# Attention rows in another order: 768 keys last, 512 keys ahead of it, the short rows between long ones

## The chip, the cores and the metric

The kernel runs on one core of one Trainium2 chip. The metric is the device time of one launch in microseconds (us); the time of a kernel is the median of its runs. The engines are TensorE (PE, with its weight loads as PEld), VectorE (DVE), ScalarE (ACT), GpSimd (POOL) and SyncE (SP).

## What is computed

Three layers run one after the other on 2 sequences of 768 positions and 512 channels: a retention with decay in blocks, a normalised two-layer MLP with 2048 inner channels, and an attention with four experts, of which a gate takes two for each position. The change lies in the last layer alone:

```python
logits = x @ w_gate
topk = np.argpartition(-logits, K, axis=-1)[..., :K]
w = np.exp(sel)                       # of the two taken, then normed
for e in range(E):
    q = x @ wq[e]
    k = x @ wk[e]
    v = x @ wv[e]
    scores = scale * (q @ k.transpose(0, 2, 1))
    scores = np.where(causal, -1000000000.0, scores)
    a = np.exp(scores)                # normed by its sum
    ye = a @ v @ wo[e]
    out += mask[..., None] * w[:, :, kk:kk + 1] * ye
```

## The kernel before

A **row** of attention is a pair (b, t): sequence b and its block t of 128 queries. Because of the causal mask row t has (t + 1) * 128 keys, from 128 (t = 0) to 768 (t = 5). There are twelve rows, and the tuple `ROWS` (line 53) names their order. Each row has four **items**, one for each expert e, so that 48 items pass through a pipeline written out by hand; TensorE's instructions stand exactly in the order in which this code gives them, while the other engines' are ordered by a scheduler.

One turn k of the last loop issues, in this order on TensorE: the scores of item k (`att_s`, L802); pieces of the filler, which are the projections of later blocks (`pv`, L744, and `pj`, L722); the transposes of item k - 5 (`att_t`, L839); in every second turn the product with v of the two items up to k - 7 (`att_av`, L851); in every fourth turn the output projection of the row whose last item is k - 10 (`att_o`, L872). Behind the last score the turns go on without scores until the last row is through.

Between the score and the transpose of an item lies work of the other engines: DVE masks the diagonal block (L804, or L809 for a pair) and takes the row maximum (L805, L811), ACT takes the exponential out of PSUM into `att` (L806, L814), DVE turns the sum into a reciprocal `c` (L825, L826), POOL multiplies by it and by the gate's weight (L829). Behind the transpose ACT copies the result out of PSUM (`aT`, L840); behind the second `av` ACT and DVE split it into two parts (`avs`, L857, L858).

Scores lie in PSUM tiles of two banks called "big", of which there are two. For rows of up to 512 keys two experts share one (a **pair**: mask, maximum and exponentials start when both scores are there); with 640 or 768 keys each expert has a tile of its own. A third tile can be begun when all readers of the first, the exponentials among them, are done:

```python
def ps_big(name):
    return psum.tile([P, 2, 512], F32, tag="big", bufs=2, name=name)
pair = n <= 512
if not pair or e % 2 == 0:
    row["s"] = ps_big(f"s{b}{t}{e}")
```

Everything else of this stage in PSUM (`pv`, `pj`, `t`, `av`, `o`) takes turns in four tiles of one bank, called "mid". The filler has 24 steps, eight for each of three blocks of queries; a row of sequence b may not start before the blocks that it reads are projected, and otherwise the steps are spread over the first 36 turns:

```python
while done < per_blk * (2 * b + t // NTB):
    more[done]()
```

One of a block's eight steps is its gate, some twenty small DVE instructions (L758 to L775).

Of the kernel before, what the change touches and what calls it, by code (L numbers as in the profile page):

```python
# [49 lines left out]
FILL = 36  # L50
AV_AT, O_AT = 2, 5

ROWS = ((0, 0), (0, 1), (0, 2), (0, 3), (0, 4), (1, 2), (0, 5), (1, 5), (1, 1), (1, 4), (1, 3), (1, 0))
LAG = 5
NG = FT // GF
E = 4
# [11 lines left out]
def model(ctx, tc, qkT, kv, lam, g_ln, w12, wat, out):  # L68
# [791 lines left out]
    def att_o(b, t):  # L860
# [3 lines left out]

        halves = 2 if (b, t) == ROWS[-1] else 1
        for j in range(halves):
# [17 lines left out]
    per_blk = len(more) // (NBLK - 1)  # L884
    items = [(b, t, e) for b, t in ROWS for e in range(E)]
    done = 0
# [77 lines left out]
```

## Time and profile before

| | |
|---|---|
| median of 3 runs | 483.04 us (483.02 to 484.16) |
| the profiled execution | 484.76 us, of which 482.8 us are the span from first to last instruction |
| PE busy | 98% of the span |
| DVE, ACT, POOL busy | 70%, 41%, 18% |
| the chain that ended last | PE 85% |

The profile is of one execution. A busy share is a mean over stages; what bounds a stage is read from the waits in it. The chain of work that ended last is followed back from the last instruction; its pieces give what each instruction added to the time.

### The profile page before, as it was taken

How to read it: one execution, taken by the hardware profiler on the slowest of the kernel's cores; microseconds unless marked ns; L12 is line 12 of the kernel's file. 1: busy time of each engine (PE TensorE's matmuls, PEld its weight loads, DVE VectorE, ACT ScalarE, POOL GpSimd, SP SyncE). 2: the span in 40 equal slices, each digit the busy share in tenths (PEclk: the TensorE clock that was granted, in tenths of full speed). 3: DMA queues.
4: the chain of work that ended last, by engine and by line, in shares of the span. 5: the costliest groups of instructions: out<-in, count | busy, mean ns of one | idle time of the engine just before them, and what ended most of it. 6: DMA issues, size and time to landing. Idle time of an engine off the chain costs nothing.

```text
span 482.8 us, 8791 instructions
## 1 busy us (share of the span) xinstructions
PE 472.1 (98%) x3451; PEld 437.9 (91%) x3456; DVE 340.3 (70%) x707; ACT 196.1 (41%) x447; POOL 85.3 (18%) x132
## 2 busy tenths in 40 slices
PE   8899999999999999999999999999999999999996
PEld 4667888999999999999999999999998889898885
DVE  4489688897999796923799925245579676676663
ACT  2326646622233332211233412022346575547672
POOL 5463430000000000000000000000045444334340
PEclk9899999999999999999999999999999999999999
DMA  7877511121334212310222400000000000000111
GB/s 279 331 223 240 196 45 45 45 87 45 113 107 128 90 56 77 98 34 1 87 88 87 132 0 1 1 1 1 0 2 0 24 23 22 24 2 23 45 44 67
DMA packets 10841, 35.18 MB, mean 73 GB/s; under 512 B 1456, under 2 KB 1712, under 8 KB 10800
## 3 DMA queue, kind: packets, MB, share of 16 engines
q1 hardware_dynamic: 10512, 34.49, 21.4%
q8 instruction: 27, 0.44, 0.4%
q10 hardware_dynamic: 288, 0.13, 0.1%
q14 instruction: 14, 0.11, 0.1%
HBM read 31.47 MB, written 3.15 MB: 72 GB/s over the span
## 4 chain that ended last, share of the span: by engine, by line
PE 85%; DVE 5%; issue 3%; DMA 3%; POOL 2%; ACT 1%; SPq 0%; POOLq 0%; DVEq 0%; ACTq 0%
PE h L485 27%; PE y L519 26%; PE pj L722 4%; PE s L802 4%; PE av L851 4%; PE o L872 4%; PE t L839 4%; PE pv L744 3%; PE yf L538 2%; DMA kvn<-in_kv 2%; PE po L373 1%; POOL qd L334 1%; PE sc L326 1%; PE po L366 1%; DMA qk<-in_qkT 1%
## 5 line engine op out<-in xcount | busy, mean ns | idle before, releaser
L485 PE MATMUL h<-xn,w 128*128 128x384 f32 x768 | 140.2, 336 | 0.0
L485 PEld LDWEIGHTS h<-xn,w 128*128 128x128 f32 x768 | 133.4, 188 | 2.8 <-issue 0.8
L519 PE MATMUL y<-hs,w 128*128 128x384 f32 x552 | 99.8, 334 | 0.0
L519 PEld LDWEIGHTS y<-hs,w 128*128 128x128 f32 x552 | 96.1, 188 | 0.0
L504 ACT ACTIVATE hs<-h 128x384 fp32r<-128x384 f32 x50 | 24.5, 490 | 101.7 <-PE h L485 88.3
L736 POOL TENSOR_SCALAR kh<-kh 64x384 fp32r<-64x384 f32 x16 | 8.4, 522 | 300.1 <-DVE qs L730 288.5
L505 DVE SCALAR_TENSOR_TENSOR hs<-h,hs 128x384 fp32r<-128x384 f32 x50 | 27.7, 554 | 41.1 <-ACT hs L504 41.1
L524 DVE TENSOR_TENSOR xT<-xT,y 128x768 f32<-128x768 f32 x30 | 28.5, 950 | 31.6 <-PE y L519 31.6
L829 POOL TENSOR_SCALAR att<-att,c,gw 128x128 f32<-128x128 f32 (+5 forms) x48 | 35.6, 747 | 51.8 <-DVE c L826 16.3
L229 ACT CAST w<-top 128x512 fp32r<-128x512 f32 x32 | 19.8, 620 | 52.3 <-DVE top L223 50.3
L722 PE MATMUL pj<-x,wa 128*128 128x384 f32 x192 | 35.0, 337 | 0.0
L722 PEld LDWEIGHTS pj<-x,wa 128*128 128x128 f32 x192 | 33.4, 188 | 0.0
L840 ACT COPY aT<-t 128x512 f32<-128x512 f32 (+3 forms) x64 | 26.6, 442 | 11.1 <-PE t L839 10.8
L839 PE MATMUL t<-ident,att 128*128 128x128 f32 x168 | 26.2, 275 | 0.5 <-DVE qs L730 0.5
L214 ACT ACTIVATE mag<-raw 128x512 f32<-128x512 f32 x32 | 21.2, 668 | 7.1 <-DVE w L241 7.1
L234 DVE SCALAR_TENSOR_TENSOR mag<-raw,mag 128x512 f32<-128x512 uint32 x32 | 23.2, 726 | 0.6
L851 PE MATMUL av<-aT,v 128*64 128x128 f32 x336 | 23.6, 280 | 0.0
L802 PE MATMUL s<-kh,qs 128*128 128x512 f32 (+3 forms) x64 | 23.3, 365 | 0.0
L238 DVE TENSOR_TENSOR top<-top,w 128x512 f32<-128x512 f32 x32 | 22.9, 715 | 0.0
L223 DVE SCALAR_TENSOR_TENSOR top<-raw,mag 128x512 int32<-128x512 int32 x32 | 21.9, 686 | 0.5
L241 DVE TENSOR_TENSOR w<-top,mag 128x512 fp32r<-128x512 f32 x32 | 21.9, 685 | 0.4
L851 PEld LDWEIGHTS av<-aT,v 128*64 128x64 f32 x336 | 17.8, 136 | 4.4 <-issue 3.9
(128 smaller groups left out, 726.8 us busy)
## 6 DMA issues: line engine op xcount, KB each, us to landing
raw<-in_w SPq DMA_DIRECT2D x32, 512.0 KB, 3.8
qk<-in_qkT SPq DMA_DIRECT2D x12, 512.0 KB, 5.5
kvn<-in_kv SPq DMA_DIRECT2D x12, 512.0 KB, 5.0
out<-os SPq DMA_DIRECT2D x11, 256.0 KB, 2.0
rawa<-in_wat SPq DMA_DIRECT2D x3, 512.0 KB, 3.3
rawa<-in_wat SPq DMA_DIRECT2D x1, 520.0 KB, 4.0
out<-os SPq DMA_DIRECT2D x1, 128.0 KB, 1.7
out<-os ACTq DMA_DIRECT2D x1, 128.0 KB, 1.7
```

Of the source, the lines that this page charges most:

```text
L234: nc.vector.scalar_tensor_tensor(mag, RAW[ft, i][:, :, 0].bitcast(U32), 2.0 ** -52, mag, ALU.mult, ALU.mult)
L485: nc.tensor.matmul(ph[:, :TB], w[:, wi, k, :], xn[:, xi, k, :], start=(i == 0), stop=(i == 11))
L504: LAST.append((nc.scalar.activation(h[:, 0], ph[:, :TB], AF.Relu), nc.vector.scalar_tensor_tensor(h[:, 1], ph[:, :TB], 0.0, h[:, 0].bitcas ...
L505: nc.vector.scalar_tensor_tensor(h[:, 1], ph[:, :TB], 0.0, h[:, 0].bitcast(F32), ALU.max, ALU.subtract)))
L519: nc.tensor.matmul(y[:, j, :TB], w[:, wi, e * P:(e + 1) * P], h[:, xi], start=(f == 0 and i == 0), stop=(f == GF - 1 and i == 2))
L524: nc.vector.tensor_tensor(xv, xv, y[:, :, :TB], ALU.add)
L722: nc.tensor.matmul(ps[:, :TB], w[:, wi, k, :], x2[:, xi, k, :], start=(i == 0), stop=(i == 11))
L802: nc.tensor.matmul(ps[:, c0:c1], q, kk[:, e, c0:c1], start=(i == 0), stop=(i == 1))
L829: nc.gpsimd.tensor_scalar(a[:, :n], a[:, :n], c, gw, ALU.mult, ALU.mult)
L839: nc.tensor.transpose(pt[:, (j - j0) * P:(j - j0 + 1) * P], a[:, j * P:(j + 1) * P], ident)
L840: nc.scalar.copy(aT[:, j0 * P:j1 * P], pt[:, :(j1 - j0) * P])
L851: nc.tensor.matmul(pav[e2 * HD:(e2 + 1) * HD, pr * P:(pr + 1) * P], v[:, j, e * HD:(e + 1) * HD], row["aT"][e][:, j * P:(j + 1) * P], star ...
```

## The change

One line: the order of the twelve rows. The first seven stay. Behind (0, 5) came (1, 5), (1, 1), (1, 4), (1, 3), (1, 0); now come (1, 1), (1, 4), (1, 0), (1, 3), (1, 5). In keys: 768, 256, 640, 512, 128 before, 256, 640, 128, 512, 768 now. The same instructions are issued on each engine, in another order.

```diff
-ROWS = ((0, 0), (0, 1), (0, 2), (0, 3), (0, 4), (1, 2), (0, 5), (1, 5), (1, 1), (1, 4), (1, 3), (1, 0))
+ROWS = ((0, 0), (0, 1), (0, 2), (0, 3), (0, 4), (1, 2), (0, 5), (1, 1), (1, 4), (1, 0), (1, 3), (1, 5))
```

**First place: turn 28, behind the scores of (0, 5).** TensorE before: (1, 5) needs sequence 1's last block of queries, so that a value step and all four projections (two query, two key) stand in a row ahead of its score `s_4465`.

```order
L839 MATMUL t_4342<-ident,att_4149 128x128 x3
L744 MATMUL pv_4347<-wa_2888,x_3_3289 128x260 x12
L722 MATMUL pj_4386<-x_3_3289,wa_2804 128x384 x12
L722 MATMUL pj_4403<-x_3_3289,wa_2841 128x384 x12
L722 MATMUL pj_4424<-x_3_3289,wa_2804 128x384 x12
L722 MATMUL pj_4441<-x_3_3289,wa_2841 128x384 x12
L802 MATMUL s_4465<-kh_3458,qs_3462 128x512
```

TensorE now: (1, 1) comes first and needs no more than is there; the value step stands in turn 28, one projection in turn 31 (`pj_4476`), three in turn 32 ahead of (1, 4)'s score `s_4566`.

```order
L802 MATMUL s_4438<-kh_3458,qs_3461 128x256
L802 MATMUL s_4438<-kl_3459,qs_3461 128x256
L722 MATMUL pj_4476<-x_3_3289,wa_2804 128x384 x12
L839 MATMUL t_4494<-ident,att_4282 128x128 x4
L839 MATMUL t_4500<-ident,att_4282 128x128 x2
L722 MATMUL pj_4504<-x_3_3289,wa_2841 128x384 x12
L722 MATMUL pj_4525<-x_3_3289,wa_2804 128x384 x12
L722 MATMUL pj_4542<-x_3_3289,wa_2841 128x384 x12
L802 MATMUL s_4566<-kh_3458,qs_3462 128x512
```

The block of five filler steps is parted into one, one and three, with scores, transposes and products between.

**Second place: the turns behind the pair of 512 keys, (1, 3) with experts 2 and 3.** TensorE before: the pair's scores are `s_4869`; then come one pair of (1, 0) in the other big tile (`s_4917`) with (1, 4)'s transposes and products, and `s_4974` is the next to need the tile of `s_4869`.

```order
L802 MATMUL s_4869<-kl_3459,qs_3462 128x512
L839 MATMUL t_4905<-ident,att_4770 128x128 x4
...
L802 MATMUL s_4917<-kh_3458,qs_3461 128x128
...
L839 MATMUL t_4929<-ident,att_4803 128x128 x4
...
L851 MATMUL av_4938<-aT_4848,v_3460 64x128
...
L839 MATMUL t_4957<-ident,att_4823 128x128 x4
L872 MATMUL o_4964<-wa_2935,avs_4894 128x512 x6
L802 MATMUL s_4974<-kh_3458,qs_3461 128x128
```

TensorE now: the pair is `s_4835`. Behind it come the transposes and the product of (1, 0), one block each, and (1, 5)'s first score `s_4877` in the other tile; (1, 5)'s second, `s_4901`, takes the tile of `s_4835`.

```order
L802 MATMUL s_4835<-kl_3459,qs_3462 128x512
L839 MATMUL t_4871<-ident,att_4732 128x128
L802 MATMUL s_4877<-kh_3458,qs_3462 128x512
...
L839 MATMUL t_4894<-ident,att_4761 128x128
L851 MATMUL av_4897<-aT_4820,v_3460 64x128
L851 MATMUL av_4897<-aT_4846,v_3460 64x128
L802 MATMUL s_4901<-kh_3458,qs_3462 128x512
```

What stands between the pair and the next user of its tile shrank from a pair of scores, fourteen transposes, ten products and an output projection to one score, two transposes and two products.

DVE now, at the same place: the mask of the pair stands behind the split `avs_4860` of row (1, 4).

```order
L826 RECIPROCAL c_4842<-c_4842 128x1
L858 TENSOR_TENSOR avs_4860<-av_4802,avs_4860 128x256
L809 COPY_PREDICATED s_4835<-tri,fill 128x2x128
L811 TENSOR_REDUCE negm_4778<-s_4835 128x2
L804 COPY_PREDICATED s_4877<-tri,fill 128x128
```

Only behind this maximum do ACT's two exponentials of the pair start.

## Rows read from the trace of the kernel before

**Rows 1.** The page: busy share of each engine; TensorE's clock in tenths, by fortieths.

```profile
PE 472.1 (98%) x3451; PEld 437.9 (91%) x3456; DVE 340.3 (70%) x707; ACT 196.1 (41%) x447; POOL 85.3 (18%) x132
PEclk9899999999999999999999999999999999999999
```

**Rows 2.** Waits of TensorE from 409 us on: us in total, times, longest.

```profile
PE o L872 <- ACT avs L857: 0.5, 1, 0.5
PE o L872 <- DVE kl L734: 0.2, 1, 0.2
```

**Rows 3.** Timeline, start and duration: output projection behind transposes, with and without wait.

```profile
433.45 0.82 PE L839 MATMUL t<-ident,att 128*128 128x128 f32 x6
434.52 1.65 PE L872 MATMUL o<-wa,avs 128*128 128x512 f32 x6 [0.25 <-DVE kl L734]
...
442.58 0.82 PE L839 MATMUL t<-ident,att 128*128 128x128 f32 x6
443.15 1.63 PE L872 MATMUL o<-wa,avs 128*128 128x512 f32 x6
```

**Rows 4.** Timeline: the pair (1, 3), experts 2 and 3, to its second exponential.

```profile
462.59 0.40 PE L802 MATMUL s<-kl,qs 128*128 128x512 f32 x1
463.03 0.44 DVE L809 COPY_PREDICATED s<-tri,fill 128x256 f32<-128x256 int32 x1 [0.30 <-PE s L802]
463.38 0.41 DVE L858 TENSOR_TENSOR avs<-av,avs 128x256 fp32r<-128x256 f32 x1
463.71 1.21 DVE L811 TENSOR_REDUCE negm<-s 128x2 f32<-128x1024 f32 x1
465.01 0.69 ACT L814 ACTIVATE att<-s,negm 128x512 f32<-128x512 f32 x1
465.69 0.68 ACT L814 ACTIVATE att<-s,negm 128x512 f32<-128x512 f32 x1
467.57 0.22 PE L802 MATMUL s<-kh,qs 128*128 128x128 f32 x1
```

**Rows 5.** Chain, start and length of a piece: the pieces that TensorE's path is made of.

```profile
436.17 0.71 PE s L802 x4
438.34 0.90 PE s L802 x4
473.55 0.11 PE t L839
475.05 0.37 PE av L851 x4
477.43 0.38 ACT avs L857
477.86 1.69 PE o L872 x12
```

**Rows 6.** Timeline of DVE in the gate: a slow one, its last.

```profile
424.11 0.70 DVE L765 TENSOR_TENSOR rank<-rank,cmp 128x9 f32<-128x9 f32 x1
428.54 0.17 DVE L775 TENSOR_TENSOR gw<-gw,mx 128x12 f32<-128x12 f32 x1
```

**Rows 7.** Timeline of TensorE around the longest wait, in the retention.

```profile
19.03 1.72 PE L326 MATMUL sc<-qk 64*128 64x128 f32 x16 [1.87 <-DMA qk<-in_qkT]
20.68 1.12 PE L357 MATMUL po<-kvn,kd 128*64 128x64 f32 x16
21.73 1.63 PE L366 MATMUL po<-qd,st 64*64 64x128 f32 x16
25.07 1.16 PE L326 MATMUL sc<-qk 64*128 64x128 f32 x16
32.13 0.69 PE L357 MATMUL po<-kvn,kd 128*64 128x64 f32 x16
32.75 1.09 PE L366 MATMUL po<-qd,st 64*64 64x128 f32 x16
```

**Rows 8.** Window of Rows 7: span, busy (count) of PE, PEld, DVE, ACT, POOL, PEclk, DMA, GB/s.

```profile
20.00:21.00 1.00, 1.00 (x14) 0.78 (x13) 0.55 (x2) 0.63 (x2) 0.67 (x1) 0.50 1.07 418
```

## The prediction, written before the changed kernel ran

> **What bounds the kernel now.** I read the page first: TensorE is busy 98% of the span and its clock is at full speed in all but one fortieth [rows 1]. The engines beside it have room (DVE 70%, ACT 41%). A mean says little about a stage, so I next took TensorE's waits from 409 us on, where the rows of attention that the change moves lie. There are two in some 70 us: 0.2 us for a `kl` of the projections and 0.5 us for the last split of all [rows 2]. The reader is to see that this stage is one unbroken stream of TensorE instructions. The change only permutes them, so their sum stays; what can differ are the waits between them. I therefore went through the new order and asked at each hand-over whether what TensorE waits for is still ready in time.
>
> **Part 1, the filler (turns 28 to 32): about 0.5 us are gained.** Before, five filler steps stand in a row. DVE clears four projections behind them, with the gate's small instructions in between, and is late by the end: the output projection that needs a freed mid tile starts 434.52 - 433.45 = 1.07 us after the transposes ahead of it, and where nothing waits the same two start 443.15 - 442.58 = 0.57 us apart [rows 3]. The wait costs 0.50 us, twice the idle time that its row shows, because the pipeline also drains. Now the gate comes two turns ahead of the first projection, and behind the last one stands a product of 24 matmuls where one of 12 stood. DVE has more time, so I take the whole 0.50 us as gained. The bounds are 0 (the wait comes back at the new place) and 0.5 us. What is late next there is the projection of turn 31: its mid tile is the one of an output projection whose copy now stands on DVE behind most of the gate's instructions, and this is a rival below. The short row (1, 1) costs nothing: its chain runs under the value step and the transposes of (0, 5).
>
> **Part 2, the pair of 512 keys ahead of the row of 768: about 2.1 us are lost.** This is the term on which the forecast hangs. There are two big tiles. The second score of (1, 5) takes the tile of the pair (1, 3) with experts 2 and 3 and cannot begin before both exponentials of that pair have left it.
>
> How long that takes, the pair's rows of before tell [rows 4]: its score ends at 462.59 + 0.40 = 462.99; mask, split and maximum follow on DVE; the exponentials end at 465.69 + 0.68 = 466.37. That is 3.38 us. Handing on to TensorE takes 0.05 us more (the last split ends at 477.43 + 0.38 = 477.81 and its user starts at 477.86 [rows 5]), together 3.43 us.
>
> What TensorE has to do meanwhile: before, 467.57 - 462.99 = 4.58 us pass until the next user of that tile [rows 4], more than 3.43, and nothing waits. Now it is a transpose of one block, a score of 768 keys, a transpose of one block and a product of one block for two experts, at 0.11, 0.71, 0.11 and 0.37 us [rows 5]: 1.30 us. The score is 0.71 where it doesn't follow a product and 0.90 where it does [rows 5]; this one follows a transpose. So TensorE stands still for 3.43 - 1.30 = 2.13 us, and no later wait is there to take it back but the last one, which stays.
>
> Its bounds: the shortest way through mask, maximum and two exponentials alone is 0.44 + 1.21 + 0.69 + 0.68 us and some 0.2 us of hand-overs, 3.2, which leaves a wait of 1.9 us. At the other end, the mask now stands behind the split of row (1, 4) on DVE, which ACT hands on only after the exponentials of the pair before; if its 0.41 us lie wholly ahead of the mask, 3.8 us and a wait of 2.5 us. I take 2.13, the measured row, since it holds the same instructions.
>
> The other hand-overs of the same kind have room. (1, 5)'s third score needs its first one's exponential, and between lie its second score, four transposes and an output projection; (1, 0) comes behind (1, 4) as (1, 3) did before, with the same pieces between.
>
> **Part 3, the drain.** The last row's chain is now that of 768 keys instead of 128, with no scores behind it to cover it. But behind its last score TensorE still has the transposes and products of (1, 3), the output projection of (1, 0) and its own first three heads' transposes. At 0.11 us for each of 26 blocks of transposes, 0.37 for each of eight blocks of products [rows 5] and 436.17 - 434.52 = 1.65 for the projection [rows 3, 5] I estimate 7.5 us. The last item's way to its transpose is, without POOL, about as long as the 3.4 us of the pair. I put it at nothing; if this cover were gone, the rest of that way would lie on the path. The sequence in the last turns, transposes, product, output projection, is the same as before, and so is the end: split, 0.5 us of waiting, the projection in two halves, the copy, the DMA. SP's and ACT's output DMAs keep their number and sizes, and the last full row's DMA is issued earlier against the end than before. Nothing is moved on SP but which row an issue writes.
>
> **The sum.** -0.50 + 2.13 = +1.6 us. The profiled execution took 484.76 us, 1.72 us above the median, and its own time would become 486.4. On the median, 483.04 us, I forecast 484.6 us. With the bounds, +1.4 to +2.5, the forecast's own range is 484.4 to 485.5.
>
> **The rivals.**
>
> *The wait takes TensorE's clock down.* In the retention TensorE stood idle for 1.87 us, and behind it the granted clock was 0.50, the level of 1.2 GHz [rows 8]. The three groups that ran from 19.03 us on took 1.72, 1.12 and 1.63 us, against 1.16, 0.69 and 1.09 us at full clock [rows 7]: 1.53 us more. The new wait is as long or longer. If the same happens, the cost is 1.6 + 1.5 = +3.1 us, 486.1 us. For it speaks the length of the wait; against it, that the matmuls around it are denser than the retention's and that shorter waits left the clock at full speed [rows 1, 2]. The Trainium skill's page "TensorE: Matmul & The Clock Gate" (Part 1: The HAM clock gate) says that there are only two rates and that an idle TensorE is taken down to the half; the trace agrees, with 0.50 behind 1.87 us. [...]
>
> *TensorE doesn't wait: the other side.* If ACT and DVE, with short rows before and after, were through with the pair in 1.30 us, or the tile were free earlier than by its second exponential, only the gain of part 1 would remain: 482.5 us, not slower than before. It decides at 1.30 + 0.50 = 1.8 us from the pair's score to its release: below that, the change is no loss. The instructions alone take 3.0 us [rows 4], which speaks against it.
>
> *The gate holds the first projection.* In turn 31 the projection needs the copy of an output projection that now stands behind some twelve of the gate's instructions on DVE. Before, the gate kept DVE until 428.7 us, with other work between, and one of its small instructions took 0.70 us where another takes 0.17 [rows 6]. The copy is due about 2.1 us after its projection ends; I reckon it to be there just in time. Two instructions so stretched would add 2 * 0.53, some 1 us to the forecast: 485.6 us.
>
> **How the numbers follow.** Chances: forecast 0.45, clock 0.30, no wait 0.15, gate 0.10. The predicted time is the forecast's, 484.6 us. The range leaves out half of the no-wait case below and a sixth or so of the clock case above: 482.7 to 486.5 us. A measurement of this kernel can tell about 0.3%, 1.45 us, from no change: below 481.6 is faster, above 484.5 slower. The forecast lies close to that edge, so a third of its chance counts as the same, with nearly all of the no-wait case: 0.15 + 0.14 = 0.29, and 0.02 for the rest, 0.31. Faster is 0.04, slower 0.65.
>
> **What would show it.** In the profile of the changed kernel: a wait of TensorE at L802 (`s` for an exponential of L814) of about 2 us, some 23 us before the end, and no other above 0.3 us but the last one; the wait at L872 for `kl` gone; the granted clock of the microseconds behind the wait, 1.00 for the forecast and 0.50 for the clock's rival; in turn 31 no wait of `pj` for the copy of L875; and transposes of the last row that wait for no POOL. I am wrong if TensorE runs through the pair without a stop, or if the last row's drain shows waits that part 3 put at nothing.

## The result, and the profile after

The changed kernel takes 486.57 us (486.10 to 486.83), the kernel before 483.03 us in the same comparison: a ratio of 1.0071, with an interval of 1.0058 to 1.0084. It is slower by 3.5 us. The forecast was 484.6 us, its range 482.7 to 486.5; the rival in which the wait takes TensorE's clock down stood at 486.1 us.

The page of the changed kernel, where the profiled execution took 486.52 us with a span of 484.5 us, answers [rows 1]: the busy share of each engine, and TensorE's clock by fortieths of the span.

```profile
PE 471.2 (97%) x3456; PEld 436.9 (90%) x3456; DVE 339.6 (70%) x707; ACT 195.7 (40%) x447; POOL 84.8 (17%) x132
PEclk9999999999999999999999999999999999999989
```

Before, the one slice below full speed was the second, in the retention; now it is the last but one, in the rows that were moved. The waits of TensorE from 400 us on answer [rows 2] (us in total, times, longest):

```profile
PE s L802 <- ACT att L814: 2.2, 1, 2.2
PE o L872 <- ACT avs L857: 0.5, 1, 0.5
```

The wait for `kl` is gone, and a score waits 2.2 us for an exponential. It is the second score of (1, 5), and the timeline shows it with the pair (1, 3) that holds its tile, as [rows 4] did (start, duration, and in brackets the idle time and what ended it):

```profile
456.72 0.39 PE L802 MATMUL s<-kl,qs 128*128 128x512 f32 x1
457.24 0.47 DVE L809 COPY_PREDICATED s<-tri,fill 128x256 f32<-128x256 int32 x1
457.74 1.22 DVE L811 TENSOR_REDUCE negm<-s 128x2 f32<-128x1024 f32 x1
457.96 0.44 PE L851 MATMUL av<-aT,v 128*64 128x128 f32 x4
459.06 0.69 ACT L814 ACTIVATE att<-s,negm 128x512 f32<-128x512 f32 x1 [0.67 <-DVE negm L811]
459.74 0.68 ACT L814 ACTIVATE att<-s,negm 128x512 f32<-128x512 f32 x1
460.56 0.50 PE L802 MATMUL s<-kh,qs 128*128 128x512 f32 x1 [2.16 <-ACT att L814]
461.75 2.91 PE L872 MATMUL o<-wa,avs 128*128 128x512 f32 x6
466.37 0.50 PE L802 MATMUL s<-kh,qs 128*128 128x512 f32 x1
```

The pair's score ends at 457.11 and its second exponential at 460.42: 3.31 us, where [rows 4] gave 3.38. TensorE has work until 457.96 + 0.37 = 458.33 (the 0.37 of [rows 5]) and goes on at 460.56: 2.23 us are lost. Behind the wait the same output projection that takes 1.63 us in [rows 3] takes 2.91. Why, the stretches of one microsecond tell (behind the busy times of PE, PEld, DVE, ACT and POOL stands TensorE's granted clock, then the DMA's share and GB/s):

```profile
461.00:462.00 1.00, 1.00 (x9) 0.95 (x8) 0.43 (x1) 0.39 (x2) 1.00 (x2) 0.85 0.00 0
462.00:463.00 1.00, 1.00 (x4) 0.81 (x4) 1.00 (x3) 0.59 (x1) 0.14 (x1) 0.50 0.00 0
...
464.00:465.00 1.00, 1.00 (x4) 0.77 (x3) 0.30 (x1) 0.36 (x2) 0.53 (x1) 0.50 0.00 0
465.00:466.00 1.00, 1.00 (x9) 0.79 (x7) 0.78 (x4) 0.00 (x0) 0.00 (x0) 0.95 0.00 0
```

From shortly before 462 us to shortly after 465 TensorE runs at 0.50, the 1.2 GHz level, and it is busy all that time: the loss does not show as a wait.

A second, smaller delay is in no list of waits of TensorE's matmuls, since it stands inside a group of transposes:

```profile
447.35 0.37 ACT L814 ACTIVATE att<-s,negm 128x128 f32<-128x128 f32 x1 [0.21 <-DVE c L826]
447.71 0.36 ACT L814 ACTIVATE att<-s,negm 128x128 f32<-128x128 f32 x1
448.06 1.06 ACT L840 COPY aT<-t 128x128 f32<-128x128 f32 x3
447.64 1.06 PE L839 MATMUL t<-ident,att 128*128 128x128 f32 x5
448.37 0.14 PEld L839 LDWEIGHTS t<-ident,att 128*128 128x128 f32 x1 [0.34 <-ACT aT L840]
448.63 0.66 PE L851 MATMUL av<-aT,v 128*64 128x128 f32 x8
...
450.53 0.71 PE L839 MATMUL t<-ident,att 128*128 128x128 f32 x5
451.17 1.31 PE L851 MATMUL av<-aT,v 128*64 128x128 f32 x20
```

Five transposes of (1, 4) with a product behind them take 448.63 - 447.64 = 0.99 us here and 451.17 - 450.53 = 0.64 further on. They need a mid tile back from an `aT` copy, which stands on ACT behind the two exponentials of (1, 0), a row that was not there before. Cost: 0.35 us.

**Where the time is compared.** The traces differ by up to 2 us ahead of the attention (in the profiled execution of before the retention ran partly at half clock [rows 7, 8]), and the code there is the same. So I compare a stretch that all kernels share: from the first score of attention to the start of the last output projection. Its ends, of before and then of after:

```profile
356.22 0.22 PE L802 MATMUL s<-kh,qs 128*128 128x128 f32 x1
```

```profile
354.33 0.22 PE L802 MATMUL s<-kh,qs 128*128 128x128 f32 x1
...
479.60 1.68 PE L872 MATMUL o<-wa,avs 128*128 128x256 f32 x12 [0.53 <-ACT avs L857]
```

Before, 477.86 [rows 5] - 356.22 = 121.64 us; after, 479.60 - 354.33 = 125.27 us; +3.63 us, close to the 3.54 us between the medians. Such a stretch is of one execution each, the profiled one.

### The profile page after: what moved, and what is told of

Same layout as the page of the kernel before. It is cut to its first block, busy times and chain, and to the rows that moved or that the text cites. A ratio compares the mean times of both kernels' runs of the same rounds, so it can differ in the third digit from the quotient of the medians.

```text
span 484.5 us, 8802 instructions
## 1 busy us (share of the span) xinstructions
PE 471.2 (97%) x3456; PEld 436.9 (90%) x3456; DVE 339.6 (70%) x707; ACT 195.7 (40%) x447; POOL 84.8 (17%) x132
## 3 DMA queue, kind: packets, MB, share of 16 engines
HBM read 31.47 MB, written 3.15 MB: 71 GB/s over the span
## 4 chain that ended last, share of the span: by engine, by line
PE 86%; DMA 4%; issue 3%; DVE 3%; ACT 2%; POOL 2%; SPq 0%; POOLq 0%; ACTq 0%; DVEq 0%
PE h L485 27%; PE y L519 26%; PE pj L722 6%; PE s L802 4%; PE av L851 4%; PE t L839 3%; PE o L872 3%; PE pv L744 3%; DMA qk<-in_qkT 2%; PE yf L538 2%; PE po L373 1%; PE po L366 1%; ACT att L814 1%; PE sc L326 1%; DMA kvn<-in_kv 1%
```

## The experiments

Stretch is the one just defined, less the 121.64 us of before. "Before" is the kernel before on the same chip in the same comparison.

| kernel | median, us | before, us | ratio (interval) | stretch, us |
|---|---|---|---|---|
| changed | 486.57 | 483.03 | 1.0071 (1.0058 to 1.0084) | +3.63 |
| seven matmuls in the wait | 484.90 | 482.91 | 1.0040 (1.0026 to 1.0054) | +2.07 |
| four | 485.14 | 482.91 | 1.0045 (1.0030 to 1.0059) | +2.05 |
| two | 485.06 | 483.11 | 1.0038 (1.0025 to 1.0051) | +2.08 |
| (1, 3) without pairs | 483.50 | 483.08 | 1.0013 (1.0004 to 1.0023) | +0.67 |
| tail 256, 128, 640, 512, 768 | 486.83 | 483.08 | 1.0071 (1.0055 to 1.0087) | +3.96 |
| tail 256, 640, 512, 128, 768 | 483.51 | 482.91 | 1.0014 (1.0001 to 1.0027) | +0.41 |
| tail 256, 768, 640, 512, 128 | 483.33 | 482.91 | 1.0009 (0.9998 to 1.0020) | +0.41 |
| 256 early, 768 not last | 483.38 | 483.08 | 1.0008 (0.9998 to 1.0018) | +0.22 |
| 256 early, 768 last | 483.92 | 483.08 | 1.0016 (1.0007 to 1.0025) | +0.97 |
| before, filler over 30 turns | 484.74 | 483.11 | 1.0028 (1.0015 to 1.0041) | +1.83 |

**The clock by itself.** If the half clock is a cost of its own behind the wait, keeping TensorE at work in the wait must give it back and leave the wait's own cost. The matmuls write a tile that nothing reads; `warm` is the kernel's own helper.

```diff
             while done < per_blk * (2 * b + t // NTB):
                 more[done]()
                 done += 1
+            if k == 45:
+                warm(7, "z")
             att_s(b, t, e)
```

> The changed kernel with seven idle matmuls on zeros (128x512, bf16) ahead of the second score of row (1, 5), in the place where TensorE waits for the pair. They belong to no result. Theory (the wait itself costs 2.2 us and the clock that falls behind it another 1.5): TensorE is kept at work for some 1.5 us of the wait, the rest of it is about 0.6 us, the score still starts when the exponentials are through, but the granted clock stays at 1.00 and the output projection behind it takes 1.6 us and not 2.9: 486.57 - 1.5 = 485.0 us. Rival (the projection behind the wait is slow for another reason, as its operands or the other engines, and the clock has no part): 486.6 us, the projection again at 2.9 us.

With seven, the clock stayed at 1.00 in every microsecond of the attention and the time fell by 486.57 - 484.90 = 1.67 us. The stretch fell by 3.63 - 2.07 = 1.56. Four of them:

> As the one with seven, but four idle matmuls: some 0.9 us of the wait are filled and TensorE stands idle for about 1.3 us in one piece. Theory, if an idle of that length leaves the clock alone: 485.0 us as with seven; if it already takes the clock down: 486.5 us with a granted clock of 0.50 behind the wait. The retention of before stood idle for 1.00 us without a fall and for 1.87 us with one, so that I put 60 to 40 on no fall. Rival (clock has no part): 486.6 us at full clock with a projection of 2.9 us.

The wait was then 1.1 us, the clock stayed at 1.00, and the stretch is the same as with seven within 0.02 us, since the exponential and not TensorE sets when the score starts. Two of them were to find the idle time at which the clock falls, after an order (below) had shown a fall behind 1.39 us:

> The changed kernel with two matmuls of no use ahead of the score that waits, so that TensorE stands idle there for about 1.6 us instead of 2.2. With four of them (1.1 us idle) the clock stayed at full speed; in the order with 128 keys ahead of 640 it fell behind an idle of 1.4 us. Theory (the idle's length decides, somewhere between 1.1 and 1.4 us): half clock behind the wait, 486.6 us. Rival (the matmuls between keep the clock up): full clock, 485.1 us.

The timeline around the wait with two:

```profile
458.71 0.11 PEld L104 LDWEIGHTS <-zeros 128*128 128x128 bf16 x2 [0.17 <-issue]
458.71 0.39 PE L104 MATMUL warmz<-zeros 128*128 128x512 bf16 x1
460.94 0.50 PE L802 MATMUL s<-kh,qs 128*128 128x512 f32 x1 [1.84 <-ACT att L814]
462.11 1.63 PE L872 MATMUL o<-wa,avs 128*128 128x512 f32 x6
...
465.18 0.50 PE L802 MATMUL s<-kh,qs 128*128 128x512 f32 x1
```

The idle time of 1.84 us in that row is too long: two weight loads stand at 458.71 and only one matmul, so the trace lacks the record of the second. In the changed kernel's retention three such matmuls take 0.82 us and one takes 0.39, so that they start (0.82 - 0.39) / 2 = 0.22 us apart. The second then ended at about 459.3, and TensorE stood idle for about 1.6 us (an estimate), as I had reckoned. That left the clock alone in all five executions (mean clock 1.000 in each), so the theory of a length between 1.1 and 1.4 us fell. This kernel and the changed one give the price of the half clock best, since they differ in the two matmuls alone: from the score that waited to the fourth score it is 466.37 - 460.56 = 5.81 us in the changed kernel and 465.18 - 460.94 = 4.24 here, 1.57 us more.

**The pair as the cause of the wait.** The order stays, but (1, 3) gives each head a tile of its own, so that the second score of (1, 5) waits for one exponential and not for two behind a common maximum.

```diff
-        pair = n <= 512
+        pair = n <= 512 and (b, t) != (1, 3)
```

(in `att_s` and in `att_c`)

> The row order of the changed kernel stays; each head of row (1, 3) has a big tile of its own instead of two heads sharing one, as the rows of 640 and 768 keys have. The second score of (1, 5) then waits for the mask, the maximum and one exponential of a single head of 512 keys (estimated 1.9 to 2.0 us) against 1.3 us of TensorE's work between. Theory (the wait is the pair's release, and the half clock follows from its length): a wait of about 0.6 us at the score, the clock at full speed behind it, and 483.0 - 0.5 + 0.6 + 0.4 = 483.5 us. Rival (the row of 768 keys as the last costs the time by itself): 485 us or more.

Timeline at the score:

```profile
458.65 0.69 ACT L806 ACTIVATE att<-s,negm 128x512 f32<-128x512 f32 x1 [0.70 <-DVE negm L805]
459.48 0.50 PE L802 MATMUL s<-kh,qs 128*128 128x512 f32 x1 [0.47 <-ACT att L806]
```

The wait is 0.47 us, the clock 1.00 throughout, and the time as expected, 483.50 us. Three of the 3.6 us are gone with the row of 768 keys still at the end and that of 512 still in front of it: that much was the price of the tile that the pair keeps and of the clock behind it, not of the order itself. A part of what is left is again a wait for an exponential, which no row of TensorE's matmuls shows: the first score of (1, 5) starts 457.57 - 457.30 = 0.27 us after the transpose ahead of it, in the changed kernel 456.97 - 456.95 = 0.02 us.

**The short row in front of the 640 keys.** Moving (1, 0) ahead puts the products of the row of 640 keys between the pair and the score that needs its tile.

```diff
-(1, 1), (1, 4), (1, 0), (1, 3), (1, 5)
+(1, 1), (1, 0), (1, 4), (1, 3), (1, 5)
```

> The row of 768 keys stays the last and that of 512 ahead of it, but the row of 128 is moved in front of that of 640: behind (0, 5) come (1, 1), (1, 0), (1, 4), (1, 3), (1, 5). Theory (each wait is the work of TensorE since the tile's last score against its readers' 3.4 us for a pair, 2.1 to 2.3 us for one head of 640): two waits, about 0.5 us at the first score of (1, 3) and about 0.4 us at the second score of (1, 5), since the products and transposes between are now those of the row of 640 keys and not of the row of 128; no half clock; gain of the filler 0.5, drain about 0.5 behind so short a wait: 484.0 us, 483.6 to 484.4. Rival (two long rows in a row at the end cost by themselves): 485 or more, with the wait of some 2 us and the half clock as in the changed kernel.

I was wrong by 2.8 us. The two waits are where they were expected, but longer, and behind the first one the clock fell (TensorE's timeline, DVE's, and a stretch of one microsecond):

```profile
446.82 0.27 PE L802 MATMUL s<-kl,qs 128*128 128x128 f32 x1
450.24 0.80 PE L802 MATMUL s<-kh,qs 128*128 128x512 f32 x1 [1.39 <-ACT att L806]
461.60 0.50 PE L802 MATMUL s<-kh,qs 128*128 128x512 f32 x1 [0.95 <-ACT att L814]
```

```profile
446.89 0.69 DVE L875 COPY os<-o 128x512 f32<-128x512 f32 x1
447.80 0.15 DVE L825 TENSOR_SCALAR c<-ssum 128x1 f32<-128x1 f32 x1 [0.23 <-ACT att L806]
448.07 0.28 DVE L804 COPY_PREDICATED s<-tri,fill 128x128 f32<-128x128 int32 x1
```

```profile
451.00:452.00 1.00, 1.00 (x7) 0.36 (x5) 0.00 (x0) 0.81 (x3) 0.87 (x1) 0.50 0.00 0
```

The head of 640 keys whose tile is wanted ends its score at 446.82 + 0.27 = 447.09, but its mask starts only at 448.07: DVE has the copy of an output projection ahead of it and, behind a short wait for ACT, the reciprocal of the head before. So the release took 450.24 - 447.09 = 3.15 us, where I had reckoned 2.1 to 2.3 from the instructions alone. Of four executions three took 486.83 to 487.11 us, with a mean clock of 0.996 over the span, and one 484.93 with 1.000. One of the three is the profiled one; for the other two the mean doesn't tell where the clock fell, but the fourth shows that the same kernel can go without the fall. Even that one is 0.9 us above the forecast.

**The row of 768 keys as the last, by itself.** Two orders end on it without 512 keys in front:

```diff
-(1, 1), (1, 4), (1, 0), (1, 3), (1, 5)
+(1, 1), (1, 4), (1, 3), (1, 0), (1, 5)
```

> Rows 512 and 128 of the changed order exchanged: ..., 256, 640, 512, 128, 768. The row of 768 keys stays last and the filler stays as changed; the pair of 128 keys now stands ahead of the 768. Theory (all of the loss is the wait for the pair of 512 and the clock behind it; the filler gains 0.5 us and the long last row costs nothing): no wait of s for an exponential above 0.3 us, clock 1.00, 483.03 - 0.5 = 482.5 us. Rival (the drain of a 768-key row at the end costs, or the order at large does): 484 us or more with waits in the last 20 us.

No score waits, but the drain does (timeline):

```profile
469.32 0.60 PE L839 MATMUL t<-ident,att 128*128 128x128 f32 x4
470.10 0.44 PE L839 MATMUL t<-ident,att 128*128 128x128 f32 x2 [0.18 <-ACT aT L840]
470.47 0.44 PE L851 MATMUL av<-aT,v 128*64 128x128 f32 x4
470.84 0.87 PE L839 MATMUL t<-ident,att 128*128 128x128 f32 x6
471.99 0.87 PE L839 MATMUL t<-ident,att 128*128 128x128 f32 x6 [0.28 <-POOL att L829]
472.79 1.53 PE L851 MATMUL av<-aT,v 128*64 128x128 f32 x24
```

The first six transposes take 470.47 - 469.32 = 1.15 us, the twelve behind 472.79 - 470.84 = 1.95; in the changed kernel six take 0.74 and twelve 1.46, without a wait:

```profile
471.27 0.82 PE L839 MATMUL t<-ident,att 128*128 128x128 f32 x6
472.01 1.09 PE L851 MATMUL av<-aT,v 128*64 128x128 f32 x16
473.04 1.53 PE L839 MATMUL t<-ident,att 128*128 128x128 f32 x12
474.50 1.53 PE L851 MATMUL av<-aT,v 128*64 128x128 f32 x24
```

The drain costs 0.41 + 0.49 = 0.90 us there. The stretch, +0.41, is that less some 0.5.

The same comparison with the row of 256 keys moved ahead of (0, 5), first with the tail of before, then with 768 keys last:

```diff
-(0, 5), (1, 1), (1, 4), (1, 0), (1, 3), (1, 5)
+(1, 1), (0, 5), (1, 5), (1, 4), (1, 3), (1, 0)
```

> The tail is that of the kernel before, (1, 5), (1, 4), (1, 3), (1, 0), but the row of 256 keys is moved ahead of (0, 5), into the stretch of the filler: ..., (1, 2), (1, 1), (0, 5), (1, 5), (1, 4), (1, 3), (1, 0). Theory (the 0.5 us of the five filler steps in a row can be had if no tile of scores is needed early anywhere): no wait of a score above 0.3 us, the wait for the projection's copy gone or kept, drain as before: 482.4 to 482.5 us, below the kernel before. Rival (the wait only moves: (0, 5)'s scores now meet the short row, or the filler's block stands in a row as before): 483.0 us or more.

```diff
-(0, 5), (1, 1), (1, 4), (1, 0), (1, 3), (1, 5)
+(1, 1), (0, 5), (1, 4), (1, 3), (1, 0), (1, 5)
```

> As the run with the row of 256 keys ahead of (0, 5), but with the row of 768 keys as the last: ..., (1, 1), (0, 5), (1, 4), (1, 3), (1, 0), (1, 5). No row of 512 keys stands directly ahead of it. The difference to that run is the price of the drain with 768 keys by itself, with no long wait ahead of it that gives the other engines time. Theory: 0.9 us of waits at the last transposes, as in the order that had 128 keys ahead of the 768: 483.4 us. Rival (the drain costs nothing, as the prediction had it): 482.5 us.

The one with 768 keys last is slower by 0.97 - 0.22 = 0.75 us in the stretch and by 0.54 between the medians, with the same two waits in the drain (0.18 and 0.27 us idle). In the one with the tail of before the rival held: the four projections still stand together ahead of a score, with two transposes between, and the wait is at its new place:

```profile
437.79 1.66 PE L872 MATMUL o<-wa,avs 128*128 128x512 f32 x6 [0.44 <-DVE kl L734]
```

**The filler's half microsecond.** Two more tries to have it without the pair. The long rows in falling order behind (1, 1):

```diff
-(1, 1), (1, 4), (1, 0), (1, 3), (1, 5)
+(1, 1), (1, 5), (1, 4), (1, 3), (1, 0)
```

> The order of before with rows 768 and 256 exchanged only: (0, 5), then 256, 768, 640, 512, 128. This is the change's filler part alone: the short row runs first, the filler is parted, the last rows stay as before. Theory: the wait of the output projection for kl is gone, 483.03 - 0.5 = 482.5 us. Rival (the wait for kl moves elsewhere, or the gate on DVE holds the first projection): 483.0 us or above, with a wait of TensorE at pj or t between 420 and 440 us.

The `kl` wait is gone, but the second score of (1, 4) now waits 0.98 us for the last exponential of (1, 5), because only the one- and two-block work of (1, 1) lies between. And the kernel before with its own order, where only the pace of the filler is changed:

```diff
-FILL = 36
+FILL = 30
```

> The kernel before with its own row order; only the filler is spread over 30 turns instead of 36, so that fewer of its steps stand in a row ahead of (1, 5). Theory (the wait at the output projection comes from the five steps in a row and costs 0.5 us): the wait for the projection's copy is gone, nothing else moves, 482.5 us, below the kernel before. Rival (more filler earlier is late somewhere else): 483.0 us or more, with another wait of TensorE in the turns before.

Timeline of TensorE's waits there:

```profile
392.12 1.65 PE L872 MATMUL o<-wa,avs 128*128 128x512 f32 x6 [0.51 <-DVE qs L730]
408.06 1.69 PE L744 MATMUL pv<-wa,x 128*128 128x260 f32 x12 [0.54 <-ACT aT L840]
415.39 1.31 PE L851 MATMUL av<-aT,v 128*64 128x128 f32 x20 [0.28 <-ACT aT L840]
```

It is slower by 1.83 us in the stretch: the wait that was removed came back as three others at earlier turns. No version beat the kernel before.

## Why the prediction was right and wrong

| step | predicted, us | measured, us |
|---|---|---|
| part 1, filler | -0.50 | -0.5, what the rest leaves |
| part 2, the wait | +2.13 | +2.23 |
| half clock | +1.53, as a rival | +1.57 |
| copies behind (1, 0) | not seen | +0.35 |
| part 3, drain | 0 | 0 |
| sum | +1.6 (rival +3.1) | +3.63 |

**Part 1 was right**, as far as a remainder can show it: 3.63 - 2.23 - 1.57 - 0.35 = -0.52 us, and the wait for `kl` is gone. The order with 128 keys ahead of the 768 agrees: its drain's 0.90 us and its +0.41 leave -0.49.

**Part 2 was right** in place, cause and size. The wait lies 24 us before the end, where some 23 were forecast; the pair's way took 3.31 us against 3.38, TensorE's work 1.22 against 1.30. The bound with the split ahead of the mask played no part: the mask started 0.13 us after the score. The run without pairs shows that the tile is the cause, since it took the wait from 2.16 to 0.47 us and changed the use of the tiles in that one row alone.

**Part 3 was right, and I had nearly talked myself out of it.** Two orders with 768 keys last did wait in the drain. But there the row in front has 128 keys, and its transposes are one block each. With 512 keys in front, from the last head's score to the last output projection it is 479.60 - 466.37 = 13.23 us in the changed kernel, and 13.23 to 13.24 in the four kernels with the same tail whose wait ahead is 0.47 to some 1.6 us long. So the cover that the prediction named is what hides the chain, not the time that the wait gives the other engines.

**The step that failed is the choice between the forecast and the clock's rival.** The forecast put the clock behind the wait at nothing; it cost 1.57 us. The rival's arithmetic was there, 1.53 us from [rows 7], and its sum of +3.1 us misses only what follows. But I gave it 0.30, against 0.45 for a clock that stays, because the matmuls around the wait are denser than the retention's and shorter waits had left the clock alone. The first reason is refuted: in the profiled execution TensorE was busy without a gap ahead of this wait and behind it, and the clock fell all the same. The other three executions were not traced; their mean clock is 0.996 too, which is what one such fall gives, but it doesn't tell where the fall lies. The second reason said nothing on a wait of this length.

One row did, 1.87 us in the retention [rows 7, 8], and it pointed to the fall; with it as the judge the forecast would have been 486.1. But that row was itself the exception. Its execution lay 1.72 us above the median, and in the experiments' comparisons only 7 of 61 executions of the kernel before have a mean clock of 0.996, the others 0.999 or 1.000, though all run through the same retention. So nothing known beforehand settled the choice, and that the rival's sum came out well doesn't show that the fall could be foreseen.

**A step was missing**: 0.35 us for the transposes whose mid tile hangs on ACT. I had followed the two big tiles through the new order, and the mid tiles only in the filler. Unrounded the rival's sum is -0.50 + 2.13 + 1.53 = +3.16 us; with this term, 0.10 more for the wait and 0.04 for the clock it becomes 3.65, against 3.63 measured. The time lies 0.07 us above the range's top.

**The other rivals.** The gate did not hold the first projection: it follows the score in turn 31 without a wait.

```profile
426.39 2.31 PE L722 MATMUL pj<-x,wa 128*128 128x384 f32 x12
```

And TensorE did wait. 1.8 us from the pair's score to its release was named as the point from which the order would be no loss; the run without pairs came near it with 459.34 - 457.46 = 1.88 us (from its score's end to its exponential's end) and a time 0.42 us above before.

## What to carry to other kernels

When rows of work are put in another order, go through every tile that rotates, the small ones too: the wait at a hand-over is the release of the tile less the work that now lies between, and a release is longer than its instructions wherever another copy stands ahead on the engine. Each order here that removed one wait made another; half a microsecond of gain is soon given back at the next tile. And where a new stop of some two microseconds falls into a stream that is bound by TensorE, cost it both ways, with the half clock behind it and without: here it cost 1.6 us on top of 2.2, and it shows in the granted clock, not in the waits.

## What was not expected of the hardware

The length of the idle time does not decide by itself whether the clock falls. In the traces it fell to 0.50 behind 2.16 us (changed kernel), 1.87 us (retention of the kernel before), 1.79 us (retention of the tail 256, 640, 512, 128, 768) and 1.39 us (the short row ahead of 640 keys). It stayed at 1.00 behind some 1.6 us (two matmuls) and, at the same place of the retention, behind 1.71 us (filler over 30 turns), 1.88 us (tail 256, 768, 640, 512, 128), 1.92 us (changed kernel) and 1.98 us (without pairs). The rows of 1.92 and of 1.88 us, and the microsecond behind the 1.92:

```profile
18.89 1.16 PE L326 MATMUL sc<-qk 64*128 64x128 f32 x16 [1.92 <-DMA qk<-in_qkT]
```

```profile
18.86 1.16 PE L326 MATMUL sc<-qk 64*128 64x128 f32 x16 [1.88 <-DMA qk<-in_qkT]
```

```profile
19.00:20.00 1.00, 1.00 (x18) 0.88 (x18) 0.97 (x2) 0.00 (x0) 0.00 (x0) 1.00 0.99 397
```

So nearly the same idle time at the same place of the code, 1.87 us in one execution and 1.88 in another, went either way. Where the clock fell, it also fell at different moments: behind the 1.39 us the first matmul was slow already (0.80 us, where others take 0.50), behind the 1.87 us some 0.4 us of work ran at full speed first (the granted clock is 1.00 up to 19.4 us and 0.63 from there to 19.6), behind the 2.16 us more than a microsecond. The prediction took from the Trainium skill's page "TensorE: Matmul & The Clock Gate" (Part 1: The HAM clock gate) that an idle TensorE is taken down to the half; for idle times of these lengths the runs show both outcomes, and they decide. The same section of the Trainium skill says that the monitor runs free of the kernel's start, so that a transition shifts from run to run. That would fit one kernel with and without the fall, but no run here shows what the monitor saw. Why two matmuls of no use were enough in all five executions, while without them the mean clock was 0.996 in all four, stays open.
